# A planner that plans again by its own latest times, with the first two layer norms' squares made later

## The chip, the cores and the metric

One core of a Trainium2 chip. The metric is the device time of one execution in microseconds, as the median of several runs: 1011.96 us before (three runs, 1010.72 to 1015.18). Tables, rows and times in the text are of that core.

## What is computed

Attention with capped scores, a feed-forward block with a layer norm ahead of it, and a gated block with a spatial product, in fp32, for 4 batches of 448 tokens and 768 features:

```python
scores = cap * np.tanh(scale * q @ k.T / cap)            # 12 heads of 64
attn = np.exp(scores - scores.max(-1)); attn /= attn.sum(-1) + 1e-09
x = attn @ v                                             # heads side by side: (4, 448, 768)
mu = x.mean(-1); var = ((x - mu) ** 2).mean(-1)
xn = (x - mu) / np.sqrt(var + 1e-06) * g_ln
x = x + np.maximum(xn @ w_ch1, 0) @ w_ch2                # 768 -> 3072 -> 768
h = np.maximum(x @ w_in, 0); u, v = h[..., :512], h[..., 512:]
v_n = (v - v.mean(-1)) / np.sqrt(v.var(-1) + 1e-06)
out = (u * (w_spatial @ v_n + b_spatial)) @ w_out
```

## The kernel before

**Numbers in two halves.** Features lie on the 128 partitions and tokens along the free side, so a batch is six tiles of 128x448. A matmul of full accuracy is three matmuls on rounded operands (fp32r): each operand is split into a first half (a copy or conversion) and a second half (the operand less its first half), and high*high, high*low and low*high are added in PSUM. Names that end in `rs` or `wh` hold such pairs. The splits are VectorE's and ScalarE's work.

**Stages.** Heads are taken in pairs. A pair has score groups in three chunks of 128 keys (matmuls `two<-qk`, two chunks and then the third), Tanh and Exp of each on ScalarE into `es`, transposed scores of the last 64 keys for two pairs at once (`bank<-qk`, `emit_st`), products with the values (`bank<-es,vt`) and sums over keys by ones (`bank<-es,ones`). VectorE adds the `es` of a pair for those sums. The sums go through DRAM to be inverted on all partitions (`invert`: DMAs `sum<-hs`, `rc<-sum`, `inv<-rc`, `hs<-inv`), then `x*R` and a running sum `acc` over the six tiles. The pairs of batches 0 and 1 come first. As soon as the acc of a batch is there, `ln_mean` sums it over the features by a pair of matmuls with ones (`bank<-wh,onesr`), and `ln_center` subtracts the mean and makes the six operands of the hidden product, `x - mean` times the gain, in two halves. A hidden unit (`h_unit`, 18 matmuls `bank<-rs,...`) is one tile of 128 hidden features of one batch. The units of batches 0 and 1 run interleaved with the pairs of batches 2 and 3; then come the second product (`y_seven`), the gated block, and the same for batches 2 and 3, some of it in seven products of halves in place of eight.

**The layer norm's scale.** The hidden units use x without its deviation; the residual is multiplied by the deviation instead (`ln_scale`: a second pair of matmuls with ones over the sum of squares, a power on GpSimd, DMAs that spread it to all partitions, six multiplications), and the reciprocal is applied after the second product. The sum of squares is made in `ln_center`, one Square on ScalarE for each tile and five additions on VectorE.

**What sets the order.** No order is written out by hand. The code records every operation with its buffers, a cost and a latency (`Recorder`, `Program.add`); `Program.order` (line 322) gives each a due time, and `Program.plan` (line 369) goes through the program in a model of time and gives every free engine the ready operation with the earliest due time for which its pools of buffers have room (`pick`). Due times: matmuls are due in the order of the code, at the sum of the costs of the matmuls ahead; others are due before their users, by cost and latency times SLACK. An operation is not taken if it is due later than the matmul cost issued so far and AHEAD = 28 (`reach`, line 406). Each engine executes its instructions strictly in the resulting order; all DMAs here are issued by SyncE. Pools that matter: two qk tiles, seven es, four PSUM banks and two double banks, ten hs, sixteen rs. Lines in profiles are 553 for all that is recorded, so rows are told apart by their tiles.

Of the kernel before, what the change touches and what calls it, by code (L numbers as in the profile page):

```python
# [44 lines left out]


AHEAD = 28
SLACK = 0.35
BIAS = 0.1
OPEN = 20.0  # L50
# [50 lines left out]
class Buf:  # L101
    def __init__(self, pool, name):
        self.pool, self.name = pool, name
        self.first = self.last = None
        self.uses = self.left = 0
        self.tile = None
        self.after = []
        self.gates = []

# [39 lines left out]
class Slots:  # L149
# [19 lines left out]
            b.left, b.tile = b.uses, None  # L169

    def take(self, b):
        b.tile = self.idle.popleft()
        self.held.add(b)
        self.changes += 1

# [43 lines left out]
class Program:  # L219
# [102 lines left out]
    def order(self):  # L322
        n = len(self.ops)
        pred = self.edges()
        self.pred, self.succ = pred, [[] for _ in range(n)]
        for i, ds in enumerate(pred):
            for j, at in ds.items():
                self.succ[j].append((i, at))
        self.bufs = []
        for i, (_, writes, reads) in enumerate(self.ops):  # L330
            mine = list(dict.fromkeys(a.buf for a in chain(writes, reads) if isinstance(a, View)))
            for b in mine:
                b.first = i if b.first is None else b.first
                b.last = i
                b.uses += 1
            self.bufs.append(mine)
        self.pools = {b.pool for m in self.bufs for b in m}
        total = 0.0
        due = [float("inf")] * n
        for i in range(n):  # L340
            engine, cost = self.ops[i][0][0][:2]
            if engine == "PE":
                due[i] = total
                total += cost
            elif i in self.soon:
                due[i] = total
        for p in self.pools:
            p.reuse()
        for s in self.stages:
            begins = [b for p in s.pools for b in p.bufs if b.first is not None]  # L350
            if s.after and begins:
                first = min(begins, key=lambda b: b.first)
                for a in s.after:
                    for b in (b for p in a.pools for b in p.bufs if not b.after):
                        assert b.last < first.first
                        b.gates.append(first)
        for i in reversed(range(n)):
            engine, cost, latency = self.ops[i][0][0][:3]
            latency += 1.4 if engine == "D" else 0.0
            for j, at in chain(self.succ[i], {(a.first, 0.0) for b in self.bufs[i] for a in b.after},  # L360
                               {(a.first, -OPEN / SLACK) for b in self.bufs[i] for a in b.gates}):
                due[i] = min(due[i], due[j] + at * SLACK - (cost + latency + self.DELAY) * SLACK)
            if due[i] == float("inf"):
                due[i] = total
        for i in self.first:
            due[i] = float("-inf")
        return self.plan(due)

    def plan(self, due):

        n = len(self.ops)
        succ, bufs = self.succ, self.bufs
        for p in self.pools:
            p.reset()
# [9 lines left out]
        out = []  # L384
# [19 lines left out]
            return False  # L404

        def reach():
            return max(spent + AHEAD, relief)

        def pick(e):

# [26 lines left out]
                heapq.heappush(q, x)  # L437
            return found

        for i in range(n):  # L440
            if not left[i]:
                release(i)
        now = 0.0
        while True:
            for e in ready:
                if busy[e]:
                    continue
                found = pick(e)
                if found is None:
                    continue  # L450
                i, k = found
                taken[i] = True
                out.append((i, k))
                for b in bufs[i]:
                    if b.tile is None:
                        b.pool.take(b)
                busy[e] = True
                cost, latency = self.ops[i][0][k][1:3]
                if e == "PE":
                    spent += cost  # L460
                free[e] = now + cost
                if e == "D":
                    moved = max(moved, now + 1.5) + latency
                    latency = moved + 0.77 - now - cost
                heapq.heappush(events, (now + cost, 0, seq, e))
                done = now + cost + latency + self.DELAY
                for j, at in succ[i]:
                    heapq.heappush(events, (max(now, done - at), 1, seq, j))
                    seq += 1
                heapq.heappush(events, (done, 2, seq, i))  # L470
                seq += 1
# [8 lines left out]
            if kind == 0:  # L480
                busy[x] = False
            elif kind == 1:
                left[x] -= 1
                if not left[x]:
                    release(x)
            else:
                for b in bufs[x]:
                    b.left -= 1
                    if not b.left:
                        b.pool.give(b)  # L490
                        if b.pool.stage is not None and not b.pool.stage.left:
                            for s in b.pool.stage.then:
                                if not s.open and all(not a.left for a in s.after):
                                    s.open = True
                                    out.append((s, None))
                                    for p in s.pools:
                                        p.changes += 1
        assert sum(k is not None for _, k in out) == n
        return out

# [60 lines left out]
def attn_ffn_gmlp_kernel(  # L561
# [104 lines left out]
    def sub(o, a, b, engines=None):  # L666

        with prog.either():
            for e in engines or (V,):
                e.tensor_tensor(o, a, b, ALU.subtract)  # L670
# [345 lines left out]
    def ln_mean(b):  # L1016
        ps = banks.get()[:, 0:S]
        feature_sum(ps, accof[b], rs if b >= 2 else wh)
        means[b] = rst[b % 2] if b >= 2 else hs.get()
        A.activation(out=means[b], in_=ps, func=ACTF.Copy, scale=1.0 / DM)  # L1020

    def ln_center(b):

        mean, sq = means.pop(b), hs.get()
        xn[b] = []
        for k in range(KD):
            u, g = hs.get(), g_t[:, k:k + 1]
            sub(u, xts[b % 2][k], mean)  # L1030
            t = rs.get()
            with prog.either():
                V.tensor_scalar(out=t[:, 0], in0=u, scalar1=g, scalar2=None, op0=ALU.mult)
                A.activation(out=t[:, 0], in_=u, func=ACTF.Copy, scale=g)
            V.scalar_tensor_tensor(out=t[:, 1], in0=u, scalar=g, in1=f(t[:, 0]), op0=ALU.mult, op1=ALU.subtract)
            xn[b].append(t)
            A.activation(out=u if k else sq, in_=u, func=ACTF.Square)
            if k:
                add(sq, sq, u)
        ln[b] = sq  # L1040
# [644 lines left out]
    def h_units(bs):  # L1685

        j0 = 0
        for m in (4, *[2] * (NF // 2 - 2)):
            w = [weight("w1", row(j0 + j)) for j in range(m)]
            mine = {}  # L1690
            for b in bs:
                for j in range(m):
                    mine[b, j] = h_unit(b, w[j])
                    if b in ln and j == 0:
                        ln_scale(b)
                    if b % 2 and j % 2:
                        h = [mine[e, i] for i in (j - 1, j) for e in bs]
# [145 lines left out]
```

## Time and profile before

| | |
|---|---|
| median of the runs | 1011.96 us |
| profiled execution | 1010.06 us, its span 1008.3 us |
| TensorE busy | 999.5 us, 99% |
| VectorE busy | 868.3 us, 86% |
| ScalarE busy | 580.5 us, 58% |
| DMA | 229.05 MB, 227 GB/s on average |
| granted TensorE clock | 1.00 throughout |

Times in rows count from the start of the span. A row of the timeline merges instructions of one form that follow each other: start, time from the first start to the last end, form and count; brackets give the idle time ahead of it and what ended that. The end of a matmul is modelled, so the distance from one start to the next is the better measure. "Busy" of the other engines is from the first to the last of an instruction's work; followers overlap by a little.

### The profile page before, as it was taken

What the parts mean: (1) busy time and instruction counts of PE and PEld (TensorE: products, weight loads), DVE (VectorE), ACT (ScalarE), POOL (GpSimd) and SP (SyncE); (2) the same over time, 40 slices, a digit from 0 to 9 for tenths busy, and PEclk for the clock granted to TensorE, in tenths of its full rate; (3) what the DMA queues carried; (4) which work ended last, traced back from release to release, by engine and by line L of the source; (5) the groups of instructions that cost most, each with busy time, mean ns of one, the idle gap of its engine ahead of it and who ended that gap; (6) DMA issues with size and microseconds to landing.
All of it is one profiled execution on the core that took longest, in us unless ns stands there. A gap on an engine that the chain in (4) does not pass through costs nothing.

```text
span 1008.3 us, 14836 instructions
## 1 busy us (share of the span) xinstructions
PE 999.5 (99%) x5060; PEld 828.4 (82%) x5060; DVE 868.3 (86%) x1472; ACT 580.5 (58%) x925; POOL 23.0 (2%) x22
## 2 busy tenths in 40 slices
PE   9999999999999999999999999999999999999998
PEld 2332788778778899999989899999999999998987
DVE  6979898878888789999869999877788988968996
ACT  8999776776667347674335355444454542314653
POOL 0000110000000000000001200000000000000010
PEclk9999999999999999999999999999999999999999
DMA  8444779999999999998044143565699867302402
GB/s 282 136 128 146 261 262 366 357 365 356 343 368 361 362 376 323 330 405 276 26 154 141 39 138 122 176 194 191 232 330 375 291 183 233 103 22 71 128 22 110
DMA packets 124848, 229.05 MB, mean 227 GB/s; under 512 B 21170, under 2 KB 93028, under 8 KB 124772
## 3 DMA queue, kind: packets, MB, share of 16 engines
q1 hardware_dynamic: 124772, 228.10, 66.0%
q8 instruction: 40, 0.66, 0.3%
q14 instruction: 36, 0.29, 0.1%
HBM read 157.48 MB, written 70.57 MB: 226 GB/s over the span
## 4 chain that ended last, share of the span: by engine, by line
PE 78%; DMA 11%; DVE 6%; ACT 3%; issue 1%; SPq 1%; DVEq 0%; ACTq 0%
PE bank L553 51%; PE two L553 26%; DMA hs<-inv 3%; DMA w<-in_w_dram 3%; DVE es L553 2%; DMA kept_w<-wc 2%; DMA rc<-sum 1%; ACT es L553 1%; SPq L553 1%; DMA inv<-rc 1%; DVE wr L553 1%; DVE hs L553 1%; ACT hs L553 1%; DMA qk<-in_qk_dram 1%; DVE x L553 1%
## 5 line engine op out<-in xcount | busy, mean ns | idle before, releaser
L553 PE MATMUL bank<-rs,wh 128*128 128x448 f32 x1728 | 361.9, 363 | 0.3 <-ACT hs L553 0.2
L553 PEld LDWEIGHTS bank<-rs,wh 128*128 128x128 f32 x1728 | 322.8, 187 | 27.5 <-issue 4.3
L553 PE MATMUL two<-rs,wh 128*128 128x448 f32 x462 | 103.4, 362 | 0.0
L553 ACT ACTIVATE rs<-hs 128x448 fp32r<-128x448 f32 x137 | 74.6, 570 | 43.0 <-DMA hs<-h 33.2
L553 DVE TENSOR_TENSOR rs<-hs,rs 128x448 fp32r<-128x448 f32 x159 | 94.2, 618 | 1.8 <-ACT rs L553 1.4
L553 PEld LDWEIGHTS two<-rs,wh 128*128 128x128 f32 x462 | 86.6, 187 | 5.8
L553 ACT ACTIVATE es<-es,capt 128x896 f32<-128x896 f32 x72 | 73.1, 1057 | 0.0
L553 ACT ACTIVATE es<-two,qsc 128x896 f32<-128x896 f32 x62 | 60.7, 1017 | 6.8 <-PE two L553 6.6
L553 PE MATMUL bank<-es,vt 128*64 128x448 f32 x288 | 62.2, 552 | 0.0
L553 DVE TENSOR_TENSOR wh<-wr,wh 128x768 fp32r<-128x768 f32 (+2 forms) x66 | 56.3, 856 | 3.8 <-ACT wh L553 3.5
L553 ACT ACTIVATE hs<-bank 128x448 f32<-128x448 f32 x62 | 33.6, 541 | 44.6 <-PE bank L553 34.5
L553 ACT ACTIVATE wh<-wr 128x768 fp32r<-128x768 f32 (+2 forms) x50 | 38.5, 770 | 28.2 <-PE bank L553 15.3
L553 DVE TENSOR_TENSOR es<-es,es 128x896 f32<-128x896 f32 x48 | 51.9, 1081 | 1.8 <-ACT es L553 1.4
L553 PEld LDWEIGHTS bank<-es,vt 128*64 128x64 f32 x288 | 17.4, 136 | 36.9 <-issue 26.7
L553 PE MATMUL two<-qk 64*128 64x448 f32 x168 | 39.9, 580 | 2.0 <-ACT es L553 2.0
L553 ACT ACTIVATE wc<-w 128x512 f32<-128x512 f32 x36 | 24.2, 674 | 30.0 <-DMA kept_w<-wc 13.3
L553 ACT ACTIVATE rs<-x 128x448 fp32r<-128x448 f32 x32 | 18.0, 574 | 37.5 <-DVE x L553 36.1
L553 PEld LDWEIGHTS two<-qk 64*128 64x128 f32 x168 | 14.1, 190 | 27.3 <-ACT es L553 15.4
L553 PE MATMUL two<-wh,rs 128*128 128x512 f32 x144 | 34.7, 390 | 0.0
L553 PE MATMUL bank<-rx,whb 128*128 128x448 f32 x144 | 32.7, 362 | 0.0
L553 PE MATMUL two<-rx,whb 128*128 128x448 f32 x144 | 32.7, 362 | 0.0
L553 DVE TENSOR_SCALAR wc<-wc 128x512 int32<-128x512 int32 x36 | 15.2, 423 | 19.3 <-ACT wc L553 19.0
(249 smaller groups left out, 1878.9 us busy)
## 6 DMA issues: line engine op xcount, KB each, us to landing
hs<-h SPq DMA_DIRECT2D x168, 224.0 KB, 5.2
h<-hx SPq DMA_DIRECT2D x84, 224.0 KB, 5.3
w<-in_w_dram SPq DMA_DIRECT2D x24, 768.0 KB, 6.8
w<-in_w_dram SPq DMA_DIRECT2D x36, 512.0 KB, 6.4
qk<-in_qk_dram SPq DMA_DIRECT2D x24, 448.0 KB, 5.1
h<-hs SPq DMA_DIRECT2D x48, 224.0 KB, 3.7
kept_w<-wr SPq DMA_DIRECT2D x24, 384.0 KB, 7.6
kept_w<-wc SPq DMA_DIRECT2D x36, 256.0 KB, 5.3
```

Source lines behind the costliest of these rows:

```text
L553: fn(*(put(a) for a in args), **{k: put(a) for k, a in kw.items()})
```

## The change

Two things. First, the planner. `order` makes the plan by the old due times, then works back through this plan from its end (`latest`): on every engine each operation must end before the latest start of the next on that engine, before its users need it, and before the next buffer in the same tile begins. These latest times become the due times of another plan, three times over; in these plans an operation is not taken if its latest time is more than WITHIN = 24 after the planner's present. Of the four plans, the one whose model ends first is made once more and issued.

Second, the squares of batches 0 and 1. `ln_center` no longer makes them. A new `ln_square` subtracts the mean from the six x tiles once more, squares and adds, right ahead of `ln_scale`; it is recorded at the first hidden unit of weight row 10 for batch 0 and of row 14 for batch 1 (of 24), where `ln_scale` was recorded with the first units of all. The mean stays in `rst` until then.

```diff
+WITHIN = 24
+ROUNDS = 3
...
-        for i in self.first:
-            due[i] = float("-inf")
-        return self.plan(due)
-
-    def plan(self, due):
+        tries = []
+        for timed in (False,) + (True,) * ROUNDS:
+            for i in self.first:
+                due[i] = float("-inf")
+            plan = self.plan(due, timed)
+            tries.append((self.end, len(tries), due, timed))
+            due = self.latest(plan)
+        _, _, due, timed = min(tries)
+        return self.plan(due, timed)
+
+    def latest(self, plan):
...
+        late = [float("inf")] * len(self.ops)
+        free = {e: self.end for e in self.engines}
+        then = [[] for _ in self.ops]
...
+        for i, k in sorted((x for x in plan if x[1] is not None), key=lambda x: -self.span[x[0]][0]):
+            e, cost = self.ops[i][0][k][:2]
+            lag = self.span[i][1] - self.span[i][0] - cost
+            t = min(chain([free[e]], (late[j] + at - lag for j, at in self.succ[i]), (late[j] - lag for j in then[i])))
+            late[i] = free[e] = t - cost
+        return late
+
+    def plan(self, due, timed):
...
-            return max(spent + AHEAD, relief)
+            return max(now + WITHIN if timed else spent + AHEAD, relief)
...
-        means[b] = rst[b % 2] if b >= 2 else hs.get()
+        means[b] = rst[b % 2]
...
-        mean, sq = means.pop(b), hs.get()
         xn[b] = []
         for k in range(KD):
             u, g = hs.get(), g_t[:, k:k + 1]
-            sub(u, xts[b % 2][k], mean)
+            sub(u, xts[b % 2][k], means[b])
...
             xn[b].append(t)
-            A.activation(out=u if k else sq, in_=u, func=ACTF.Square)
+
+    def ln_square(b):
...
+        mean, sq = means.pop(b), hs.get()
+        for k in range(KD):
+            u = hs.get() if k else sq
+            sub(u, xts[b % 2][k], mean)
+            A.activation(out=u, in_=u, func=ACTF.Square)
             if k:
                 add(sq, sq, u)
         ln[b] = sq
...
-                    if b in ln and j == 0:
+                    if j0 == 10 + 4 * b and j == 0:
+                        ln_square(b)
                         ln_scale(b)
```

Three places show what the order makes of it. Numbers that are left in names are those of the built program's buffers; `_420` and `_421` are the two qk tiles.

TensorE, from the third score chunk of head pair 11 (the first row) to the transposed scores of pairs 12 and 13 (64x448 from both qk tiles), before:

```order
L553 MATMUL two_142<-qk_421 128x448 x2
L553 MATMUL bank_137<-es_415,vt_0_422 64x448 x2
L553 MATMUL bank_137<-hs_82,vt_0_422 64x448
L553 MATMUL bank_137<-hs_83,vt_0_422 64x448
L553 MATMUL bank_138<-es_413,ones_124 64x448 x2
L553 MATMUL bank_139<-qk_420 64x448
L553 MATMUL bank_140<-qk_420 64x448
L553 MATMUL bank_139<-qk_421 64x448
L553 MATMUL bank_140<-qk_421 64x448
L553 MATMUL bank_138<-es_416,vt_0_423 64x448 x2
L553 MATMUL bank_138<-es_414,vt_0_423 64x448 x2
L553 MATMUL two_141<-qk_420 128x448 x2
```

and now:

```order
L588 MATMUL two_142<-qk_421 128x448 x2
L588 MATMUL bank_137<-es_415,vt_0_422 64x448 x2
L588 MATMUL bank_137<-hs_87,vt_0_422 64x448
L588 MATMUL bank_137<-hs_82,vt_0_422 64x448
L588 MATMUL bank_140<-es_413,ones_124 64x448 x2
L588 MATMUL bank_139<-es_416,vt_0_423 64x448 x2
L588 MATMUL bank_139<-es_414,vt_0_423 64x448 x2
L588 MATMUL two_141<-qk_420 128x448 x2
L588 MATMUL two_142<-qk_420 128x448 x2
L588 MATMUL bank_138<-qk_420 64x448
L588 MATMUL bank_140<-qk_420 64x448
L588 MATMUL bank_138<-qk_421 64x448
```

The transposed scores went behind the next pair's first value products and its first two score chunks, which need the other qk tile alone.

SyncE, the loads around the second of these qk tiles (`qk_421`); `hs<-inv` spreads an inverse of a head pair, before:

```order
L553 DMA hs_84<-inv_2_156 64x448 x2
L553 DMA hs_86<-inv_2_156 64x448 x2
L553 DMA qk_421<-in_qk_dram 128x896
L553 DMA sum_6_157<-hs_87 4x448
L553 DMA vt_0_422<-in_v_dram 128x2x192
L553 DMA vt_0_422<-in_v_dram 64x2x64
```

and now:

```order
L588 DMA qk_421<-in_qk_dram 128x896
L588 DMA rc_91<-sum_6_157 128x14
L588 DMA w_427<-in_w_dram 128x1536
L588 DMA inv_2_156<-rc_90 128x14
L588 DMA vt_0_422<-in_v_dram 128x2x192
L588 DMA vt_0_422<-in_v_dram 64x2x64
L588 DMA sum_8_159<-hs_85 2x448
L588 DMA inv_6_158<-rc_91 128x14
L588 DMA hs_84<-inv_2_156 64x448 x2
```

The qk load went ahead of the four inverse loads, and these behind eight other DMAs.

VectorE, while batch 0's operands are made (`hs<-x,...` subtracts the mean, `rs` are the halves, `hs_79` in before is the sum of squares), before:

```order
L553 SCALAR_TENSOR_TENSOR rs_68<-hs_80,g_t,rs_68 128x448
L553 TENSOR_SCALAR rs_69<-hs_88,g_t 128x448
L553 RECIPROCAL rc_90<-rc_90 128x14
L553 TENSOR_TENSOR hs_79<-hs_79,hs_87 128x448
L553 TENSOR_TENSOR hs_81<-x_3_115,hs_85 128x448
L553 TENSOR_TENSOR hs_79<-hs_79,hs_80 128x448
L553 TENSOR_TENSOR es_413<-es_418,es_417 128x896
L553 SCALAR_TENSOR_TENSOR rs_70<-hs_81,g_t,rs_70 128x448
L553 SCALAR_TENSOR_TENSOR rs_69<-hs_88,g_t,rs_69 128x448
L553 TENSOR_TENSOR es_413<-es_413,es_415 128x896
L553 TENSOR_TENSOR hs_79<-hs_79,hs_81 128x448
L553 TENSOR_TENSOR es_413<-es_413,hs_82 64x448
```

and now:

```order
L588 TENSOR_SCALAR rs_68<-hs_80,g_t 128x448
L588 TENSOR_SCALAR rs_69<-hs_88,g_t 128x448
L588 SCALAR_TENSOR_TENSOR rs_68<-hs_80,g_t,rs_68 128x448
L588 TENSOR_TENSOR es_413<-es_418,es_417 128x896
L588 SCALAR_TENSOR_TENSOR rs_69<-hs_88,g_t,rs_69 128x448
L588 TENSOR_TENSOR es_413<-es_413,es_415 128x896
L588 COPY hs_79<-bank_139 128x448
L588 TENSOR_TENSOR es_413<-es_413,hs_87 64x448
L588 TENSOR_TENSOR es_413<-es_413,hs_82 64x448
L588 TENSOR_TENSOR hs_81<-x_4_116,rstd_135 128x448
L588 COPY x_3_121<-bank_138 128x448
```

The sums of squares are gone from here, the subtraction reads the mean from `rstd`, and two copies out of PSUM stand here. In the whole order VectorE has 20 instructions more, ScalarE 7 fewer and GpSimd one fewer. On TensorE the two pairs of matmuls with ones over the squares stand among the later hidden units instead of ahead of and behind batch 1's first one; apart from that and from the place above, its order differs at a few places only.

## Rows read from the trace of the kernel before

**Rows 1.** The page's first part: busy us, share of span, instructions of each engine.

```profile
PE 999.5 (99%) x5060; PEld 828.4 (82%) x5060; DVE 868.3 (86%) x1472; ACT 580.5 (58%) x925; POOL 23.0 (2%) x22
```

**Rows 2.** Busy time in stretches: length, engines (instructions), clock, DMA share, GB/s.

```profile
75.00:100.00 25.00, 23.73 (x114) 7.30 (x112) 24.37 (x44) 24.91 (x38) 0.00 (x0) 1.00 0.46 143
125.00:975.00 850.00, 849.72 (x4349) 753.87 (x4348) 736.74 (x1248) 454.95 (x747) 19.21 (x12) 1.00 0.69 238
150.00:300.00 150.00, 149.78 (x839) 115.90 (x839) 127.11 (x202) 104.33 (x148) 1.04 (x1) 1.00 1.01 359
```

**Rows 3.** Timeline of TensorE from 79 to 127 us: start, us, group, idle before.

```profile
79.71 0.98 PE L553 MATMUL bank<-qk 64*64 64x448 f32 x8
80.62 0.97 PE L553 MATMUL bank<-es,vt 128*64 128x448 f32 x4
...
83.16 1.77 PE L553 MATMUL two<-qk 64*128 64x448 f32 x8
...
86.52 1.02 PE L553 MATMUL two<-qk 64*128 64x448 f32 x4
87.47 0.97 PE L553 MATMUL bank<-es,vt 128*64 128x448 f32 x4
...
90.63 2.00 PE L553 MATMUL bank<-qk 64*64 64x448 f32 x4
92.87 0.97 PE L553 MATMUL bank<-qk 64*64 64x448 f32 x4 [0.24 <-DMA qk<-in_qk_dram]
93.77 1.72 PE L553 MATMUL bank<-es,vt 128*64 128x448 f32 x8
95.42 1.77 PE L553 MATMUL two<-qk 64*128 64x448 f32 x8
98.15 1.02 PE L553 MATMUL two<-qk 64*128 64x448 f32 x4 [0.95 <-ACT es L553]
...
101.51 3.88 PE L553 MATMUL bank<-rs,rs 128*128 128x448 f32 x18
...
112.42 0.41 PE L553 MATMUL bank<-wh,onesr 128*128 128x448 f32 x1
113.02 0.47 PE L553 MATMUL bank<-wh,onesr 128*128 128x448 f32 x1 [0.19 <-DVE wh L553]
113.33 3.77 PE L553 MATMUL bank<-rs,wh 128*128 128x448 f32 x18
116.94 0.57 PE L553 MATMUL bank<-wh,onesr 128*128 128x448 f32 x2
117.44 1.77 PE L553 MATMUL two<-qk 64*128 64x448 f32 x8
...
123.41 3.87 PE L553 MATMUL bank<-rs,rs 128*128 128x448 f32 x18
```

**Rows 4.** Timeline of TensorE near the end.

```profile
988.62 0.57 PE L553 MATMUL two<-rs,rbc 128*128 128x448 f32 x2
...
992.40 1.36 PE L553 MATMUL two<-rs,wh 128*128 128x448 f32 x6
```

**Rows 5.** Timeline of SyncE's DMA issues around 88 us.

```profile
86.34 2.40 SPq L553 DMA_DIRECT2D hs<-inv  x4
88.83 0.54 SPq L553 DMA_DIRECT2D qk<-in_qk_dram  x1
```

**Rows 6.** The page's DMA issues: count, KB each, median us to landing.

```profile
qk<-in_qk_dram SPq DMA_DIRECT2D x24, 448.0 KB, 5.1
```

**Rows 7.** ScalarE's groups from 66 to 140 us: form, count, busy us, mean ns.

```profile
L553 ACT ACTIVATE hs<-hs 128x448 f32<-128x448 f32 x12 | 6.4, 570 | 0.0
```

**Rows 8.** VectorE's groups from 66 to 140 us.

```profile
L553 DVE SCALAR_TENSOR_TENSOR rs<-hs,g_t,rs 128x448 fp32r<-128x448 f32 x12 | 7.7, 672 | 0.0
L553 DVE TENSOR_TENSOR hs<-x,hs 128x448 f32<-128x448 f32 x12 | 7.1, 616 | 0.0
L553 DVE TENSOR_TENSOR hs<-hs,hs 128x448 f32<-128x448 f32 x10 | 6.1, 611 | 0.0
```

More of the change, by code (lines that the diff above doesn't have):

```diff
@@ L105, in __init__ @@
         self.uses = self.left = 0
-        self.tile = None
+        self.tile = self.tile_at = None
         self.after = []
@@ L171, in take @@
     def take(self, b):
-        b.tile = self.idle.popleft()
+        b.tile = b.tile_at = self.idle.popleft()
         self.held.add(b)
@@ L364, in order @@
                 due[i] = total
-        for i in self.first:
-            due[i] = float("-inf")
-        return self.plan(due)
-    def plan(self, due):
+        tries = []
[11 more added lines that the diff above has]
+        then = [[] for _ in self.ops]
+        users, holds = {}, {}
+        for i, k in plan:
+            if k is None:
+                continue
+            for b in self.bufs[i]:
+                t = id(b.tile_at)
+                if holds.get(t) is not b:
+                    for j in users.get(t, ()):
+                        then[j].append(i)
+                    holds[t], users[t] = b, []
+                users[t].append(i)
+        for i, k in sorted((x for x in plan if x[1] is not None), key=lambda x: -self.span[x[0]][0]):
[5 more added lines that the diff above has]
+    def plan(self, due, timed):
         n = len(self.ops)
+        self.span = [None] * n
         succ, bufs = self.succ, self.bufs
@@ L438, in pick @@
             return found
+        now = 0.0
         for i in range(n):
@@ L442, in plan @@
                 release(i)
-        now = 0.0
         while True:
@@ L466, in plan @@
                 done = now + cost + latency + self.DELAY
+                self.span[i] = now, done
                 for j, at in succ[i]:
@@ L497, in plan @@
                                         p.changes += 1
+        self.end = now
         assert sum(k is not None for _, k in out) == n
```

## The prediction

> **What bounds the kernel now.** I read the page's busy line first [rows 1]: TensorE is busy 999.5 of 1008.3 us, VectorE 868.3, ScalarE 580.5. So only time in which TensorE waits can be won. The windows view says where that is [rows 2]: from 125 to 975 us TensorE is busy 849.72 of 850.00 us at a granted clock of 1.00, so that stretch offers nothing. From 75 to 100 us it is 23.73 of 25.00, and there VectorE and ScalarE are full as well: they work 24.37 and 24.91 us of the 25.00.
>
> Busy TensorE time is not all work, since a group that waits in its middle shows as a long group. So I measured from start to start in the timeline [rows 3]. A transposed-score group (8 matmuls bank<-qk) takes 0.91 us where nothing holds it (79.71 to 80.62), but 3.14 from 90.63 to 93.77: 2.23 us too long, and the row inside it names the load of qk. The value products and sums of a head pair take 2.54 us (80.62 to 83.16), but 3.16 from 87.47 to 90.63: 0.62 too long. A score group of two chunks takes 1.77 by its own row at 95.42, but the next starts 2.73 later: 0.96, waiting for ScalarE's es. The two matmuls of batch 1's mean take 0.91 (112.42 to 113.33) against 0.50 for the same pair at 116.94: 0.41, waiting for VectorE's second half wh. Together 4.22 us. Batch 0's first hidden unit starts at 101.51, batch 1's at 123.41. The last wait is near the end [rows 4]: 12 matmuls take 3.78 us from 988.62 to 992.40, where 18 of the same shape take 3.61 from 113.33 on, 0.20 each: 1.38 us too long.
>
> **The change, part by part.** (1) *The transposed scores of head pair 12.* Their second tile is loaded into the slot that the third score chunk of the pair before (86.52 to 87.47) leaves. In before the load stands on SyncE's queue behind four loads of an inverse; those go out from 86.34 for 2.40 us and the qk load is issued at 88.83 [rows 5], 1.4 us after the slot is free; TensorE has only the 2.54 us group before it needs the tile, and it goes on at 92.87, 5.40 after the release. In the new order TensorE first has that group, then the next pair's first products (93.77 to 95.42 in before, 1.65) and two score chunks (1.77): 5.96 us, and the load no longer stands behind the inverses. 5.96 covers 5.40 with 0.5 to spare, and 0.4 if the load takes the 5.1 us of its median [rows 6] and is issued 0.5 after the release. I take the whole 2.2; bounds 0 and 2.23. "DMA: Bandwidth & Descriptors" of the Trainium skill (section on the anatomy of one DMA) gives, from a fit on another issue path, about 2.0 us plus the bytes at 436 GB/s, which would be an estimated 3.1 us for 448 KB; by that the cover would be ample. The median of 5.1 in this trace is longer, and it decides: the cover is thin.
>
> (2) *The squares.* The lines taken out of the centring are 12 squares on ScalarE, 6.4 us, and 10 sums on VectorE, 6.1 us [rows 7, 8]; half of each is batch 0's and stands in front of its first hidden unit, 3.2 and 3.1 us of two engines that are full there. What they held up is the 0.62, the 0.96 and the 0.41. The new order also gives VectorE three copies there that ScalarE had, about 1.9 us at the 616 ns of a subtraction of that shape, so VectorE is eased by 1.2 us alone, ScalarE by some 5. I take the whole 0.96, which waits for ScalarE, and half of the other 1.03: 1.5 us; bounds 0 and 1.99.
>
> (3) *What is late next.* Batch 1's first unit needs the mean, then six subtractions (616 ns) and six second halves (672 ns) on VectorE [rows 8], 7.7 us, plus about 1.1 for ScalarE's mean and the first hand-over: 8.8 from the start of the mean's second matmul to the last half. That half is read by the 17th of 18 matmuls, 3.2 us into the unit, so the unit can start 5.6 after it. Cover on TensorE is 5.97 (117.44 to 123.41, the same groups in both orders) plus 0.3. In before the squares' work stood between, but so did a fourth unit and another pair of matmuls as cover. VectorE's foreign rows in the chain (conversions of weights, 0.4 to 0.7 each) can use up the 0.7 that is left. I take a new wait of 0.4; bounds 0 and 2.5, for up to four foreign instructions at VectorE's means.
>
> (4) *What comes back later.* Twelve subtractions anew at 616 ns are 7.4 us of VectorE; the sums, conversions and the two matmul pairs come too. The pairs are TensorE's in any place: 0.50 each, no gain, no loss. In 150 to 300 us VectorE is busy 127.11 of 150.00, so 22.9 us are idle [rows 2]. What comes into that stretch and did not stand there is 7.4 + 6.1 + about 2.4 (four more of some 0.6 each around the two pairs of matmuls) = 15.9. It fits and nothing reads its result before the second product adds to x, after all the hidden units, so I cost it at nothing. If the cover were gone, each pair of matmuls would wait for its sum: the queue of one VectorE conversion and one sum, 1.2 us a pair, 2.5 in all.
>
> (5) *The tail.* Its matmuls stand in the same order, and the same VectorE halves are waited for: 0 of the 1.38; bounds a gain of 1.38 and a loss of 1.4.
>
> Sum: 2.2 + 1.5 - 0.4 = 3.3 us less than the profiled execution's 1010.06 (a span of 1008.3 and 1.8 around it), so 1006.8. The median of the runs shown, 1011.96, lies 1.9 above the profiled one; I carry that over: 1008.7.
>
> One rule speaks for far more. TensorE's weight loads are busy 82% [rows 1], in 75 to 100 us only 7.30 of 25.00. "Perfetto Trace Analysis" of the Trainium skill (section Identifying the Most-Contended Engine) says that matmul occupancy misleads and that the share of weight loading shows the headroom. By that, some 18% of the span would be open, and most of 75 to 100 us. The rows do not bear it out: the fp32 groups there follow each other at constant distances with no idle time between, and a faster feeder would not shorten them.
>
> **Rivals.** *A larger gain.* Besides (1) and (2) whole, with no new wait (4.2), the tail's 1.38 goes as well: 5.6, so 1004.5 profiled and 1006.4 as a median. For it: latest times are worked back from the plan's end, so the last groups are where they bind most. Against: the order of the tail's matmuls is as it was.
> *The gain moves on.* The load is covered by only 0.5 us and the chain of (3) has 0.7. If the load is 1.5 us late and the chain takes its 2.5, the gain is about 0, 1010.06 profiled, 1012.0 as a median. For it: a unit cannot pass another on TensorE's queue. Against: VectorE has less to do in the chain than before.
> *Slower: VectorE's idle time in 150 to 300 us can't be used.* Part (4) asks for 15.9 of 22.9 us, in an in-order queue whose idle bits stand where its inputs are late. Whatever is not taken up delays the halves of weights and scores that TensorE needs next, one for one. It outweighs the gain from 3.3 us on; if six tenths are not taken up, 9.5 us, the result is 1016.3 profiled, 1018.2 as a median. For it: VectorE carries 20 instructions more in the whole order, ScalarE 7 fewer. Against: TensorE did not wait in this stretch, 149.78 of 150.00 busy, and ScalarE has 45 us of room.
> *The new planning changes nothing that counts:* the orders agree except for renamed buffers. Against it stand the moved rows of TensorE and SyncE in the section on the change. 1012.0.
>
> **How the numbers follow.** A measurement of this kernel tells about 0.5% (5 us) from no change. Chances: forecast 0.58, larger gain 0.13, gain moves on 0.18, slower 0.08, nothing 0.03. Forecast, moved on and nothing lie within 0.5%; of the larger gain I count nearly all as faster, since its 5.6 is just past 5, of the slower rival nearly all as slower. Faster 0.12, same 0.81, slower 0.07. The range: the larger gain and 1.5 below it (the runs shown lie up to 1.2 under their median) down to 1004.8; upward 1013.5, the gain gone with 1.5 on top. The forecast's own range is 1006.5 to 1011.
>
> **What would show it.** (1) The group bank<-qk near 92 takes about 0.9 us from start to start and no row names DMA qk. (2) No ACTIVATE hs<-hs before 125 us, ScalarE idle for several us in 75 to 100, batch 0's first hidden unit starting near 98 (101.51 in before). (3) Batch 1's first unit near 119.6, with less than 0.5 of idle time before it. (4) From there to 975 us TensorE busy as in before, the two wh,onesr pairs among the hidden units without a wait. (5) 1.4 us of waits at the end. It is wrong if the first unit of batch 1 starts later than 121.5, or if idle time of TensorE shows between 150 and 970.

## The result: 1.1% slower, and the profile after

The changed kernel takes 1022.59 us (median of six runs, 1020.50 to 1028.83) beside 1012.22 for the kernel before (six runs, 1010.72 to 1016.43): a ratio of 1.0109, with a 95% interval of 1.0084 to 1.0134. The forecast was 1008.7, the range 1004.8 to 1013.5. The profiled execution took 1020.50 us, its span 1018.7 against 1008.3. The helper's line is L588 now and was L553.

The page's busy line of the changed kernel answers to [rows 1], and the windows to [rows 2] (length, then busy us of TensorE, weight loads, VectorE, ScalarE, GpSimd, then granted clock, DMA share, GB/s):

```profile
PE 1001.6 (98%) x5060; PEld 829.7 (81%) x5060; DVE 876.5 (86%) x1492; ACT 579.5 (57%) x918; POOL 16.5 (2%) x21
```

```profile
75.00:100.00 25.00, 25.00 (x133) 9.53 (x130) 21.69 (x40) 24.19 (x33) 0.00 (x0) 1.00 0.45 134
100.00:125.00 25.00, 21.93 (x101) 15.18 (x100) 21.48 (x38) 13.86 (x23) 0.00 (x0) 0.93 0.70 211
125.00:975.00 850.00, 842.42 (x4294) 746.52 (x4294) 739.76 (x1255) 456.25 (x745) 14.52 (x11) 1.00 0.70 239
150.00:400.00 250.00, 243.58 (x1314) 197.19 (x1313) 212.31 (x344) 165.01 (x248) 3.24 (x2) 0.99 0.99 348
250.00:275.00 25.00, 21.99 (x116) 16.74 (x115) 21.23 (x38) 14.95 (x25) 0.00 (x0) 0.93 0.89 296
```

The work is the same: 5060 matmuls, and VectorE and ScalarE about as full. From 75 to 100 us TensorE now has no idle time, as forecast. From 125 to 975 it is busy 842.42 of 850.00, where [rows 2] has 849.72, and in two stretches the granted clock is 0.93.

TensorE's timeline of the changed kernel (answers to [rows 3, 4]; brackets: idle time ahead of the row and what ended it):

```profile
93.16 0.98 PE L588 MATMUL bank<-qk 64*64 64x448 f32 x8
...
97.43 4.11 PE L588 MATMUL bank<-rs,rs 128*128 128x448 f32 x18
...
108.58 3.77 PE L588 MATMUL bank<-rs,wh 128*128 128x448 f32 x18
115.41 1.40 PE L588 MATMUL bank<-wh,onesr 128*128 128x448 f32 x2 [3.06 <-ACT wh L588]
116.74 2.79 PE L588 MATMUL two<-qk 64*128 64x448 f32 x8
...
123.73 3.88 PE L588 MATMUL bank<-rs,rs 128*128 128x448 f32 x18
...
185.07 0.57 PE L588 MATMUL bank<-rs,rs 64*128 64x448 f32 x4
188.30 1.48 PE L588 MATMUL bank<-rs,wh 128*128 128x448 f32 x6 [2.66 <-ACT hs L588]
...
260.15 0.98 PE L588 MATMUL bank<-qk 64*64 64x448 f32 x8
264.14 5.48 PE L588 MATMUL bank<-rs,wh 128*128 128x448 f32 x18 [3.01 <-ACT hs L588]
...
373.89 0.47 PE L588 MATMUL bank<-rs,wh 128*128 128x448 f32 x1 [0.56 <-ACT rs L588]
...
745.49 0.88 PE L588 MATMUL bank<-rs,wh 128*128 128x448 f32 x3 [1.12 <-ACT hh L588]
...
999.49 1.39 PE L588 MATMUL two<-rs,rbc 128*128 128x448 f32 x6
...
1002.84 0.96 PE L588 MATMUL two<-rs,wh 128*128 128x448 f32 x4
```

The bookkeeping, from start to start. Batch 0's first hidden unit starts at 97.43, 4.08 earlier than in [rows 3]; the transposed scores at 93.16 take 0.91 (the next group starts at 94.07). Batch 1's first unit starts at 123.73, 0.32 later than before: all of it is gone. The unit at 108.58 is followed after 6.83 us instead of 3.60 (3.2 too long), the ones pair after 1.33 instead of 0.50, the score group of 8 matmuls after 2.72 (to 119.46) instead of 1.77. Behind that come 0.5 for the ones pair of batch 0's squares, which in [rows 3] still stood ahead of that unit, at 116.94, and the waits at 188 (2.7 too long from start to start, by what the same two groups take in run 11 below, 181.54 to 182.03), at 264 (3.1, and 1.8 more because the 18 matmuls after it take 5.41, to 269.55, instead of 3.60), at 373 (1.3) and at 745 (1.3): the waits make 10.2 us. The tail gives back 0.4 (999.49 to 1002.84 is 3.35, in [rows 4] 3.78). The sum, 0.3 + 0.5 + 10.2 - 0.4 = 10.6, is close to the 10.4 by which the span grew.

Who is late? ScalarE's timeline of the changed kernel just ahead of three of these waits:

```profile
111.51 0.68 ACT L588 ACTIVATE wc<-w 128x512 f32<-128x512 f32 x1 [5.79 <-DVE acc L588]
113.56 0.91 ACT L588 ACTIVATE wr<-w 128x768 f32<-128x768 f32 x1 [1.37 <-DMA w<-in_w_dram]
...
114.79 0.57 ACT L588 ACTIVATE wh<-acc 128x448 fp32r<-128x448 f32 x1
...
186.29 0.89 ACT L588 ACTIVATE wr<-w 128x768 f32<-128x768 f32 x1 [4.13 <-DMA w<-in_w_dram]
...
187.62 0.62 ACT L588 ACTIVATE hs<-bank,qsc 128x448 f32<-128x448 f32 x1
...
262.53 0.66 ACT L588 ACTIVATE wc<-w 128x512 f32<-128x512 f32 x1 [5.03 <-DMA kept_w<-wc]
...
263.56 0.52 ACT L588 ACTIVATE hs<-bank 128x448 f32<-128x448 f32 x1
```

Each time ScalarE stands at the conversion of raw weights (`wr<-w`, `wc<-w`), and close behind it, in its own order, stands what TensorE waits for: the mean's first half (`wh<-acc`) or PSUM evictions (`hs<-bank`). Two of the brackets name something other than the raw load. For the row at 111.51 the load landed at 111.40; that it waited for `acc` is an inference of the profile, and run 11 below, in the same order, starts this conversion before that `acc` is made and names the load. For the row at 262.53 the raw load landed at 261.72 and the store that is named at 262.43.

At the first wait the `acc` itself is late too. VectorE's rows of the changed kernel, then SyncE's issue of what it waits for:

```profile
109.81 1.16 DVE L588 TENSOR_TENSOR x<-x,hs 128x448 f32<-128x448 f32 x2 [2.04 <-DMA hs<-inv]
...
112.42 0.62 DVE L588 TENSOR_TENSOR acc<-acc,x 128x448 f32<-128x448 f32 x1
```

```profile
104.21 1.22 SPq L588 DMA_DIRECT2D hs<-inv  x2
```

The `acc` is ready at 113.04, in the kernel before at 110.38; there the last inverses went out between 97.84 and 102.28.

### The profile page after: what moved, and what is told of

Same layout as the page of the kernel before. It is cut to its first block, busy times and chain, and to the rows that moved or that the text cites. A ratio compares the mean times of both kernels' runs of the same rounds, so it can differ in the third digit from the quotient of the medians.

```text
span 1018.7 us, 14879 instructions
## 1 busy us (share of the span) xinstructions
PE 1001.6 (98%) x5060; PEld 829.7 (81%) x5060; DVE 876.5 (86%) x1492; ACT 579.5 (57%) x918; POOL 16.5 (2%) x21
## 2 busy tenths in 40 slices
DMA packets 124848, 229.05 MB, mean 225 GB/s; under 512 B 21170, under 2 KB 93028, under 8 KB 124772
## 4 chain that ended last, share of the span: by engine, by line
PE 78%; DMA 11%; ACT 4%; DVE 4%; SPq 1%; issue 1%; ACTq 0%; DVEq 0%
PE bank L588 50%; PE two L588 28%; DMA kept_w<-wc 3%; DMA w<-in_w_dram 2%; DMA h<-hx 2%; ACT es L588 2%; SPq L588 1%; ACT hs L588 1%; DMA hs<-std 1%; DVE es L588 1%; DVE x L588 1%; DMA wr<-kept_w 1%; DMA inv<-rc 1%; DMA vt<-in_v_dram 1%; DVE wh L588 0%
## 5 line engine op out<-in xcount | busy, mean ns | idle before, releaser
L588 PE MATMUL bank<-rs,wh 128*128 128x448 f32 x1728 | 364.7, 364 | 7.5 <-ACT hs L588 5.7
L588 PEld LDWEIGHTS bank<-rs,wh 128*128 128x128 f32 x1728 | 323.9, 188 | 36.7 <-ACT hs L588 7.5
L588 PE MATMUL two<-rs,wh 128*128 128x448 f32 x462 | 103.5, 362 | 0.0
L588 DVE TENSOR_TENSOR rs<-hs,rs 128x448 fp32r<-128x448 f32 x159 | 94.5, 621 | 2.3 <-ACT rs L588 2.0
L588 PEld LDWEIGHTS two<-rs,wh 128*128 128x128 f32 x462 | 86.5, 187 | 6.3 <-ACT hs L588 0.4
L588 ACT ACTIVATE rs<-hs 128x448 fp32r<-128x448 f32 x131 | 72.2, 570 | 33.4 <-DMA hs<-h 30.4
L588 ACT ACTIVATE es<-es,capt 128x896 f32<-128x896 f32 x72 | 72.9, 1052 | 0.0
L588 ACT ACTIVATE es<-two,qsc 128x896 f32<-128x896 f32 x62 | 60.6, 1012 | 8.4 <-PE two L588 7.0
L588 PE MATMUL bank<-es,vt 128*64 128x448 f32 x288 | 62.2, 552 | 0.0
L588 DVE TENSOR_TENSOR wh<-wr,wh 128x768 fp32r<-128x768 f32 (+2 forms) x66 | 56.6, 857 | 3.4 <-ACT wh L588 3.1
L588 ACT ACTIVATE hs<-bank 128x448 f32<-128x448 f32 x59 | 31.7, 540 | 39.4 <-PE bank L588 33.4
L588 DVE TENSOR_TENSOR es<-es,es 128x896 f32<-128x896 f32 x48 | 52.1, 1086 | 0.5 <-ACT es L588 0.5
L588 PEld LDWEIGHTS bank<-es,vt 128*64 128x64 f32 x288 | 17.5, 136 | 36.7 <-issue 30.4
L588 ACT ACTIVATE rs<-x 128x448 fp32r<-128x448 f32 x33 | 18.6, 576 | 49.8 <-DVE x L588 49.8
L588 ACT ACTIVATE wh<-wr 128x768 fp32r<-128x768 f32 (+2 forms) x45 | 35.4, 786 | 16.9 <-PE bank L588 7.8
L588 PE MATMUL two<-qk 64*128 64x448 f32 x168 | 41.0, 594 | 1.1 <-ACT es L588 1.1
L588 ACT ACTIVATE wc<-w 128x512 f32<-128x512 f32 x36 | 24.4, 679 | 29.1 <-DMA kept_w<-wc 11.8
L588 PEld LDWEIGHTS two<-qk 64*128 64x128 f32 x168 | 14.6, 196 | 26.9 <-ACT es L588 18.3
L588 PE MATMUL two<-wh,rs 128*128 128x512 f32 x144 | 34.7, 390 | 0.0
L588 PE MATMUL two<-rx,whb 128*128 128x448 f32 x144 | 32.7, 362 | 0.0
L588 PE MATMUL bank<-rx,whb 128*128 128x448 f32 x144 | 32.7, 362 | 0.0
L588 ACT ACTIVATE hx<-bank 128x448 f32<-128x448 f32 x35 | 18.9, 540 | 23.2 <-PE bank L588 23.1
```

The source lines that it names most:

```text
L588: fn(*(put(a) for a in args), **{k: put(a) for k, a in kw.items()})
```

## The experiments

The first four runs set theory A (planning by latest times alone is at fault) against B (the later squares alone are at fault). After them stood C: the order before was chosen out of many by its constants, and any other meets transfers later than its planner thinks. The first four runs had 1011.92 us for the kernel before (seven runs).

**1. The later squares alone.**

```diff
-ROUNDS = 3
+ROUNDS = 0
```

> The squares are made later as in the change, but the plan is the one by the old due times (no round by latest times). Theory A, that the plan by latest times costs the time (it puts conversions that wait for a load ahead of what TensorE needs on ScalarE's queue): no waits of 2.7 and 4.9 us at 185 and 260 us, time 1008 to 1012 us, ratio 0.995 to 1.001. Theory B, that the later squares cost it (more work for VectorE, ScalarE and the DMA queue between 150 and 300 us): the waits of the changed kernel between 150 and 300 us stay, time at least 1017 us.

1021.11 us, ratio 1.0083 [1.0054, 1.0113].

**2. Planning by latest times alone.** The squares are back in `ln_center`; the first plan by latest times is taken, whatever the model says of it.

```diff
-        _, _, due, timed = min(tries)
+        _, _, due, timed = tries[1]
...
-    def ln_square(b):
...
+            A.activation(out=u if k else sq, in_=u, func=ACTF.Square)
```

> The squares stay where they were; the plan by the latest times of the first round is taken whatever the model says of it. Theory A: slower than before by 5 to 15 us, with waits of 1 us and more after 100 us in which ScalarE stands at a conversion that waits for a load. Theory B: as before, within 3 us.

1030.16 us, ratio 1.0176 [1.0152, 1.0200]. Each half alone is about as slow as both together (run 1) or slower (run 2), so neither A nor B can stand alone. TensorE's waits by what ended them (us in total, times, longest) in run 1, then in run 2:

```profile
PE bank L588 <- DVE wh L588: 6.0, 6, 2.0
PE bank L588 <- ACT hs L588: 4.4, 3, 2.5
```

```profile
PE bank L588 <- ACT wh L588: 4.5, 3, 2.6
PE two L588 <- ACT es L588: 3.2, 3, 2.2
```

Each order waits at other places for other things.

**3. All DMAs due 8 us earlier in the latest-times plan.**

```diff
+LEAD = 8.0
...
-        _, _, due, timed = min(tries)
+        _, _, due, timed = tries[1]
...
+        for i, (alts, _, _) in enumerate(self.ops):
+            if alts[0][0] == "D":
+                late[i] -= LEAD
```

> The change, with every DMA's latest time moved 8 us ahead before the second plan is made, and that plan taken. Theory A in its narrow form (the loads are planned too late): the waits at 185 and 260 us are gone and the time is 1014 us or less. Theory A in its wide form (any order by latest times leaves TensorE's inputs no slack): about as the change, 1018 to 1025 us.

1030.00 us, ratio 1.0168 [1.0142, 1.0194]: no cure, and above both expected ranges. It is once more a new order, with many small waits (the longest for ScalarE's `hx` 1.8 us) and one for a `qk` load:

```profile
PE bank L592 <- DMA qk<-in_qk_dram: 2.9, 1, 2.9
```

**4. A planner that thinks every transfer takes 2 us longer.**

```diff
-                    latency = moved + 0.77 - now - cost
+                    latency = moved + 2.77 - now - cost
```

> The change, with 2 us more latency for every DMA in the planner's model, so that the order keeps that much room for loads; of the four plans that the planner makes by this model it takes the third (latest times, second round). Theory A, narrow: 1014 us or less, since a load that lands 2 to 3 us later than the old model says no longer holds ScalarE. Theory A, wide: 1017 to 1025 us. Theory B: 1017 us or more, since the squares are as late.

1025.51 us, ratio 1.0131 [1.0097, 1.0165]. From 150 to 400 us TensorE hardly waits any more (249.09 busy of 250), but a `qk` load alone now holds it for 5.3 us near 118:

```profile
150.00:400.00 250.00, 249.09 (x1349) 202.28 (x1348) 218.84 (x355) 159.39 (x240) 2.76 (x2) 1.00 0.99 341
```

```profile
PE bank L588 <- DMA qk<-in_qk_dram: 5.3, 1, 5.3
```

Re-planning changes the order and the waits at once, so the next runs leave the order as it is and change the transfers.

**5 and 6. Half of the weights' bytes, in the changed order and in the order before.** The planner still reckons with the whole transfer.

```diff
+    def half(o, i, n, key=None):
+        def call():
+            a, b = (x.place() if isinstance(x, View) else x for x in (o, i))
+            k = key or a.tensor.name
+            m = n // 2 if full.get(k, 0) >= n else n
+            full[k] = max(full.get(k, 0), m)
+            nc.sync.dma_start(out=a[:, 0:m], in_=b[:, 0:m])
+        prog.ops[-1][0][0][3][:] = [call]
...
+            half(t, full["d", n], n)
...
+            half(raw.rearrange("p n t -> p (n t)"), source[kind][j].bitcast(I32), 2 * n)
...
+                full.setdefault(("d", n), d)
+                half(d, t, n, ("store", n))
```

> The changed kernel, every instruction in the changed order, but each transfer of weights (raw weights in, remade weights out and in again, except w2's remade ones) moves only half of its columns once its buffer has been filled; the other half of the buffer keeps older weights, so the product is of other numbers. Theory C (in any new order ScalarE stands somewhere at a weight whose transfer is late, with evictions behind it that TensorE waits for): the waits of 3.06 us at 115, 2.66 at 188 and 3.01 at 264 us shrink to under 1 us each, the slow-clock groups at 116 and 264 take 1.77 and 3.6 us again, and the time falls from about 1022 to 1011-1015 us. Rival B (the order on TensorE and VectorE is itself worse, transfers play no part): the waits stay within 0.5 us, 1020-1025 us.

> The kernel before with the same halved weight transfers (half of the columns of each is not moved). Theory C and rival B: TensorE did not wait for transfers between 125 and 975 us, so 1009-1013 us, at most the 2.2 us of the qk wait at 92 us less. If half the bytes made anything faster by itself (less contention for the other transfers or for SBUF), it shows here as well: below 1007.

The changed order falls from 1022.59 to 1010.40 us (1008.07 to 1012.28, ten runs), the order before to 1009.84 (1008.57 to 1011.16; its ratio to the kernel before is 0.9981 [0.9968, 0.9994]). So 12 us of the changed kernel hang on the bytes of the weights' transfers, and 1.4 of the kernel before. Against the kernel before, the changed order is at 0.9990 [0.9977, 1.0004]. Theory C holds here, the time a little under its range; the rival named in the expectation falls. The windows of run 5, then of run 6:

```profile
75.00:100.00 25.00, 25.00 (x133) 9.08 (x130) 22.41 (x39) 24.22 (x33) 0.00 (x0) 1.00 0.42 125
100.00:125.00 25.00, 23.55 (x118) 17.61 (x117) 22.73 (x41) 15.89 (x25) 0.00 (x0) 1.00 0.58 174
150.00:400.00 250.00, 249.81 (x1353) 203.22 (x1352) 219.84 (x356) 171.13 (x260) 6.39 (x2) 1.00 0.87 284
```

```profile
75.00:100.00 25.00, 23.73 (x114) 7.23 (x112) 24.75 (x44) 24.91 (x38) 0.00 (x0) 1.00 0.49 146
100.00:125.00 25.00, 25.00 (x128) 18.87 (x125) 22.75 (x41) 19.74 (x34) 3.00 (x1) 1.00 0.63 192
150.00:400.00 250.00, 250.00 (x1358) 204.51 (x1357) 211.16 (x335) 163.47 (x243) 0.00 (x0) 1.00 0.87 289
```

The waits between 150 and 400 us are gone and the clock is 1.00 throughout. What is left of the change is the prediction's rival "the gain moves on": 1.27 us of TensorE's time won from 75 to 100, 1.45 lost from 100 to 125.

**7 and 8. Other orders of the same old work.** AHEAD 27 instead of 28; SLACK 0.36 instead of 0.35, in the kernel before.

```diff
-AHEAD = 28
+AHEAD = 27
```

```diff
-SLACK = 0.35
+SLACK = 0.36
```

> The kernel before with AHEAD 27 instead of 28 (how far beyond the work already given to TensorE the planner looks for work for the other engines): no new rule, no moved squares, the same instructions, but a good part of VectorE's and ScalarE's instructions in other places. Theory C (before's order is the lucky one of many, and any other order has waits the planner does not see): 1016-1025 us, with TensorE waits of 1 us and more between 125 and 970 us, most of them with ScalarE waiting for a transfer just before. Rival (only latest-times planning or the moved squares cost time): 1010-1014 us.

> The kernel before with SLACK 0.36 instead of 0.35 (by which the durations are scaled when due times are set): a second order of the same work, other than that with AHEAD 27. Theory C: 1014-1025 us, with waits at other places than in the run with AHEAD 27. Rival: 1010-1014 us.

1016.36 us (ratio 1.0049 [1.0030, 1.0068]) and 1013.06 (1.0014 [1.0000, 1.0028]): slower both, the second just clear of no change; the first inside what C expected, the second below it and inside its rival's range. So not every new order costs 8 to 18 us. The order before is one of the better ones rather than the only good one. Both have TensorE waits of their own between 150 and 450 us (the longest 2.2 and 1.7 us) for what ScalarE makes.

**9 and 10. The halved transfers in the orders of runs 2 and 1.** The edit is that of runs 5 and 6. The theory is now called D: the DMA engines are full from 150 to 400 us (over this stretch a share of 1.01 before and 0.99 in the changed kernel, with 0.89 from 250 to 275, where TensorE stood still).

> The kernel planned anew by latest times without the later squares (1030.2 us in its own run), with the halved weight transfers (half of the columns of each isn't moved). Theory D (from 150 to 400 us the DMA engines are busy all the time, DMA share 0.95 to 1.04 in both kernels, so in an order that was not fitted to them a transfer lands too late somewhere and ScalarE or VectorE stands before it with TensorE's operands behind): 1009-1015 us. Rival (this order's loss of 18 us lies in the order on TensorE, VectorE and ScalarE, and only the changed kernel's happened to lie in transfers): 1022-1030 us.

> The later squares with the old due times (1021.1 us in its own run), with the halved weight transfers (half of the columns of each isn't moved). Theory D: 1007-1012 us, and, compared with 1009.8 of the kernel before with halved transfers, this is what the later squares are worth when transfers are out of the way: by the prediction's steps 1 to 3 about 3 us less, so 1007. Rival: 1018-1022 us.

Run 9: 1021.60 us (1018.34 to 1028.28), 8.6 less than run 2, but far above the 1009 to 1015 that D expected. This order also waits for `es` (3.1 us) and for VectorE's halves (`wh`, 1.9) with all transfers early; D explains nearly half of its loss of 18, the rest lies in the order on the other engines, as the rival said. Run 10: 1008.80 us, 12.3 less than run 1. Against run 6 the later squares under the old planner are worth about 1 us (the ratios to the kernel before are 0.9967 [0.9953, 0.9981] and 0.9981 [0.9968, 0.9994]; the intervals overlap), not the 3 that were expected. Run 10's waits tell where the rest went:

```profile
PE bank L588 <- DVE wh L588: 3.3, 4, 1.2
```

**11. Only the raw weights' loads halved, in the changed order.** Of the edit of run 5 only the raw load's line stays.

> The changed kernel with only the raw weights' loads halved (half of their columns isn't moved); the remade weights go out and come in whole. If the raw loads' bytes are what makes transfers late (they are 8 bytes for a weight, the remade ones 4): 1010-1014 us, with no TensorE wait over 1.5 us between 125 and 970 us. If the remade weights' transfers matter as much (ScalarE's 5.03 us wait at 262.53 names the store of one): 1015-1019 us, with the wait at 264 us still there.

1009.69 us (1007.24 to 1013.26), ratio to the kernel before 0.9974 [0.9958, 0.9990]: all of the gain of run 5. The remade weights' stores are whole here, although the row at 262.53 above names one. ScalarE's timeline in run 11 has the conversions of 186.29 and 262.53 with no wait ahead of them. The one of 111.51 still waits 2.89 us for its load, but both conversions are done before `acc` is there (111.60). TensorE's shows the units behind the former waits, and the second half of batch 1's mean as the wait that is left:

```profile
108.80 0.68 ACT L588 ACTIVATE wc<-w 128x512 f32<-128x512 f32 x1 [2.89 <-DMA w<-in_w_dram]
...
111.64 0.58 ACT L588 ACTIVATE wh<-acc 128x448 fp32r<-128x448 f32 x1 [0.59 <-DVE acc L588]
...
178.30 0.89 ACT L588 ACTIVATE wr<-w 128x768 f32<-128x768 f32 x1
...
255.51 0.68 ACT L588 ACTIVATE wc<-w 128x512 f32<-128x512 f32 x1
```

```profile
113.80 0.47 PE L588 MATMUL bank<-wh,onesr 128*128 128x448 f32 x1 [1.06 <-DVE wh L588]
114.20 1.77 PE L588 MATMUL two<-qk 64*128 64x448 f32 x8
...
182.03 8.28 PE L588 MATMUL bank<-rs,wh 128*128 128x448 f32 x40
...
260.63 3.88 PE L588 MATMUL bank<-rs,wh 128*128 128x448 f32 x18
```

**12. One eighth more of raw weights, in the order before.**

```diff
+    def more(i, m):
+        d = dram.tile([128, m], I32, name=f"more_{len(prog.ops)}")
+        prog.ops[-1][0][0][3].append(lambda: nc.sync.dma_start(out=d[:], in_=i[:, 0:m]))
...
+            more(source[kind][j].bitcast(I32), n // 4)
```

> The kernel before, its order unchanged, with one more transfer behind each load of raw weights: an eighth of the same weights once more, into a place in DRAM that nothing reads. Theory D: the DMA engines have no room from 150 to 400 us, so what they get in addition comes later, ScalarE and VectorE wait for weights and TensorE for them: 1018-1040 us, TensorE waits only between 150 and 450 us. Rival (the DMA engines are busy because nothing stops the loads from running ahead, and have room; only the order counts): 1010-1014 us.

1031.99 us (1029.81 to 1033.25), ratio 1.0195 [1.0165, 1.0225]. The window of 150 to 400 us, in the kernel before and then in run 12:

```profile
150.00:400.00 250.00, 249.72 (x1356) 204.09 (x1355) 210.10 (x334) 162.66 (x240) 1.04 (x1) 1.00 1.01 361
```

```profile
150.00:400.00 250.00, 237.11 (x1267) 189.86 (x1266) 193.43 (x308) 149.69 (x217) 3.58 (x1) 0.99 1.00 349
```

TensorE loses 12.6 us there and 0.5 from 400 to 975; most of the rest of the 20 us is longer busy time (1006.4 us in all, 999.5 before) at a mean granted clock of 0.997. ScalarE converts 46 raw tiles in that window (below), so about 28 x 64 KB + 18 x 96 KB = 3.6 MB came on top, an estimate of 10 us at 349 GB/s: the transfers are the bound of this stretch as much as TensorE is. The run also gives SyncE 76 DMAs more to issue; what that costs apart from the bytes was not measured (runs 5 and 11 leave the number of DMAs as it is). "DMA: Bandwidth & Descriptors" of the Trainium skill (Specifications; Where 436 GB/s comes from) gives about 358 GB/s as HBM's share for a core and 425 measured for a core alone with 16 MB transfers. The trace of the kernel before has 361 over this stretch at a DMA share of 1.01, near the lower figure; but from 425 to 450 us it has 407 at 1.03, so neither figure alone says here when the engines are full, and the share does.

ScalarE's groups of raw conversions from 150 to 400 us, last the idle time ahead of them and what ended it; the kernel before, the changed one, run 11, run 12:

```profile
L553 ACT ACTIVATE wc<-w 128x512 f32<-128x512 f32 x28 | 18.9, 674 | 24.6 <-DMA kept_w<-wc 11.9 <-DMA w<-in_w_dram 11.0 <-DMA vt<-in_v_dram 1.6
L553 ACT ACTIVATE wr<-w 128x768 f32<-128x768 f32 x18 | 16.0, 912 | 4.8 <-DMA kept_w<-wr 2.9 <-DVE es L553 1.4 <-DMA w<-in_w_dram 0.5
```

```profile
L588 ACT ACTIVATE wc<-w 128x512 f32<-128x512 f32 x28 | 19.0, 679 | 21.5 <-DMA kept_w<-wc 11.8 <-DMA w<-in_w_dram 7.6 <-DMA vt<-in_v_dram 1.0
L588 ACT ACTIVATE wr<-w 128x768 f32<-128x768 f32 x17 | 15.5, 911 | 7.1 <-DMA w<-in_w_dram 4.7 <-DMA kept_w<-wr 1.6 <-DVE wr L588 0.7
```

```profile
L588 ACT ACTIVATE wc<-w 128x512 f32<-128x512 f32 x27 | 18.2, 675 | 0.1
```

```profile
L553 ACT ACTIVATE wc<-w 128x512 f32<-128x512 f32 x29 | 19.4, 671 | 41.8 <-DMA kept_w<-wc 24.1 <-DMA w<-in_w_dram 14.6 <-DVE rs L553 2.2
```

This is the case in four views. ScalarE stood idle ahead of these conversions as long before as after, most of it for weights coming in or going out: 24.6 + 4.8 = 29.4 us, and 21.5 + 7.1 = 28.6. TensorE lost 0.3 us in this stretch before, now 6.4. What changed is what stands behind the waiting instruction.

## Why the prediction was wrong

**Steps (1) and (2), the two gains, were right up to batch 0's first unit.** The `qk` wait is gone, no square stands ahead of that unit, and it starts at 97.43 where "near 98" was forecast. One sign did not come: ScalarE was to be idle for several us from 75 to 100 and was busy 24.19 of 25.00, in a stretch that holds 133 matmuls now and 114 in [rows 2].

**Step (3), the new wait at batch 1's first unit, failed: it began its chain too late.** Forecast 0.4, bound 2.5; that unit starts at 123.73, not 119.6, and past the 121.5 that was named as a refutation. The step counted VectorE's work from the mean's second matmul on, and there no wait came. The time went at the mean itself, whose inputs the step took to be there: from 108.58 on 3.2 us were lost ahead of the ones pair, and 1.8 more behind its start. Of the 3.2, about 1.5 are the late `acc` (113.04). The loads of the inverses are among what the new order moved back on SyncE's queue, and step (1) had counted the move of the `qk` load ahead of them as a gain alone. Another 1.7 passed until the mean's first half began at 114.79: two weight conversions stand ahead of it on ScalarE, and the second one's load was late. Of the 1.8, 0.95 are the score group at the low clock; the rest lies in the pair, whose second matmul waited for VectorE's second half as well. In run 11 `acc` is ready 1.4 earlier, the pair starts on time, and the wait for that second half is what remains (from the pair's start to the score group 1.83 us instead of 0.50).

**Step (4), "what comes back later costs 0", failed, and carries the sign.** It looked for a stretch of idle VectorE time and found 22.9 us. VectorE did take the work: 129.27 of 150.00 us busy from 150 to 300, and 136.05 in run 5, where [rows 2] has 127.11. Hardly any TensorE wait in the changed kernel names it. The stretch was full in another column of the same row: a DMA share of 1.01 in [rows 2], which the argument never used. In a stretch where transfers are full, moving instructions of ScalarE and SyncE changes which transfer lands last and what stands behind it; that cost 2.7 + 3.1 + 1.8 us at 188 and 264, and runs 5 and 11 take exactly these away. "Perfetto Trace Analysis" of the Trainium skill (section Optimization Strategy) says that the most-contended engine can change from regime to regime of a kernel; the traces agree: a DMA share of 0.46 from 75 to 100 us [rows 2], 1.01 from 150 to 400. The causes of the 1.3 us each at 373 and 745 were not isolated: run 5 keeps a wait at both places, 0.2 us at the first and 1.1 at the second. Against the forecast, 4.1 us of the error lie ahead of batch 1's first unit, in step (3), and 10.2 behind it, in step (4).

**Step (5), the tail, was right:** 0.4 gained of a bound of 1.4.

**The rivals.** The slower one had the right sign and the wrong place: VectorE's idle time. VectorE's halves did come late in other orders (6.0 us in run 1, 3.3 left in run 10; 3.1 and 4.1 in runs 2 and 3, the former without the later squares), not in the changed kernel. "The gain moves on" is what is left once weights arrive in time. Its 1012.0 was written for the whole change, though, and that is refuted. The general mistake was to list as movable only what the diff names, and to hold all other instructions' order for as good as before.

**Open.** Why run 2's order still loses nearly 10 us with halved transfers (run 9) was not pursued. How much of the late `acc` lies in SyncE's order and how much in slow transfers was not taken apart. That the order before was chosen by its constants is argued from runs 7 and 8, which are slower by 0.5% and 0.14%; two draws show that it is a good one, not how rare it is. No version beat the kernel before with whole transfers.

## What to carry to other kernels

In a planned order, look at every resource column of the stretch where work is moved, the DMA share first; where it stands near 1.0, as here, an order is worth no more than the arrival of its loads lets it be. A wait that costs nothing today is not slack: ask what stands behind it in its queue, and count it as a bound of any change that shuffles that queue. To tell an order's own worth from its transfers, keep the order and halve the bytes; one such run did more than four new plans.

## What the runs showed of the hardware

Two waits of TensorE were followed by slow matmuls: after 3.06 us of idle time a score group of 8 took 2.79 instead of 1.77 us, after 3.01 us 18 matmuls took 5.48 instead of 3.77, and the granted clock was 0.93 over these 25 us (0.50 from 115.40 to 116.74, 0.62 from there to 119.46), so part of each ran at 1.2 instead of 2.4 GHz. After the wait of 2.66 us at 188 the window's clock stayed at 1.00. Either wait of 3 us cost nearly 5 in this kernel; in the first, some of that is the wait for VectorE's second half.

The two directions were not alike. Taking away 21 MB of raw weights (229.05 MB moved by the changed kernel, 208.08 in run 11) saved 13 us of the changed kernel and, in the order before, halving raw and remade weights together saved 1.4; adding 5.9 MB (234.95 in run 12) cost the kernel before 20 us. It has no TensorE wait for weights and no room for more of them either.
